# A's scores first, their maximum subtracted by VectorE: a scheduling change in a fused Nyström attention and SiLU layer

## The chip, the cores and the metric

The kernel runs on one core of a Trainium2 chip. A core has five engines with a queue each, and each works its queue in order: TensorE (PE; its weight loads are shown apart, as PEld), VectorE (DVE), ScalarE (ACT), GpSimd (POOL) and SyncE (SP). They meet at semaphores. Matrix products go to PSUM, 8 banks of 128 partitions x 2 KB, and VectorE and ScalarE fetch them from there. The metric is the device time of one execution in microseconds (us).

## The reference

Eight batches of eight heads, 576 tokens, 64 numbers a head. Keys and queries are averaged over 18 tokens each to 32 landmarks; three softmaxes come out of them, and the pseudo-inverse of the small one is found by six Newton steps. Heads are then joined to rows of 512, and one hidden layer of 2048 with SiLU follows:

```
q_lm, k_lm = mean over 18 tokens of q, k          # 32 landmarks a head
A  = softmax(scale * q    @ k_lm.T)               # 576 x 32
Bm = softmax(scale * q_lm @ k_lm.T)               # 32 x 32
C  = softmax(scale * q_lm @ k.T)                  # 32 x 576
Z  = Bm.T / (norm_1(Bm) * norm_inf(Bm) + 1e-6)
six times: Z = 2 Z - Z @ Bm @ Z
x  = A @ Z @ C @ v                                # heads joined: 4608 x 512
h  = x @ w_in;  out = (h / (1 + exp(-h))) @ w_out # 512 -> 2048 -> 512
```

## The kernel before, in words

The kernel is a hand-written order of instructions: what stands first in the program stands first in its engine's queue. It walks over batches b = 0 to 7, each in 16 steps s. In every step the hidden layer of batch b advances: `l1(s)` computes two blocks of 128 hidden columns for half of the tokens ("hps", four matmuls of 288 columns into one of two double banks), `act(s)` is ScalarE's SiLU from "hps" to "gT", and `l2_mm(n)` issues n matmuls of the output layer ("ops", 128x512). Sixteen of them make one output tile of 128 tokens; the sixteenth is followed by ScalarE's copy "ost" and a store from SP's queue. The tables CNT, EVEN and ODD say how many are issued in each step of batches 0 and 1, of even and of odd batches; they are the filling between the other work.

In the same 16 steps the attention of batch b + 1 is prepared by an object `a` (class Att). From b = 2 on this runs so:

- step 1: B's scores into columns 448 to 511 of a bank "bb" (`b_scores`), C's scores into both double banks "scp" (`c_scores`), their maxima on VectorE, the table of the exponential on ScalarE, and B's exponential `b_exp` ("pb");
- step 2: A's scores in five chunks of up to 128 tokens, two to a bank (`a_scores(0)`, `(1)`, `(2)`). `a_max` on VectorE writes the negated maximum of each row and head to "nm"; `a_shift` adds it to the scores by a matmul with the identity; `a_exp` on ScalarE writes the exponentials. Between them stand pieces of `l2_mm`. The last chunk has 64 tokens. At the end comes the table of SiLU;
- step 3: two pending `act`, the first products of the Newton steps (`f_mm`, `ns_mm`), which go on to step 8, one a step, with VectorE's part `ns_step`;
- step 6: C times v (`w_mm`), scaled into W; GpSimd multiplies A by its reciprocal sums, and SP's queue transposes it by DMA ("AT");
- steps 10 to 14: `z_mm` gives Z C v per head, and `m_pair` multiplies it by w_in ("mb"), the weights of the next batch's `l1`.

The first tile of A's scores lies in the one bank of the pool "a" (`psa1`, also used by `m_pair` and `w_mm`), the second in one of the two banks of pool "o" that "ops" uses, the third in columns 128 to 383 of "bb". GpSimd's queue loads q and k well ahead of their use (`load_qk`), one transfer for four heads of q or k, forms landmark sums, and copies the landmarks into block-diagonal form (`bd_expand`, in step 15).

Helpers record most instructions, so many have the line of a helper: every matmul has L77. The lines the text speaks of: L273 B's maximum, L286 B's exponential, L349 the first Newton scaling, L420 and L425 C's maximum and its scaling, L430 C's exponential, L545 A's maximum, L558 A's exponential, L651 and L652 the copies of `m_pair`, L685 SiLU, L711 "ost", L151 a change of ScalarE's table.

Of the kernel before, what the change touches and what calls it, by code (L numbers as in the profile page):

```python
# [8 lines left out]
FP = mybir.dt.float32  # L9
# [31 lines left out]
def kernel(  # L41
# [34 lines left out]
    def mm(o, lhsT, rhs, start, stop):  # L76
        nc.tensor.matmul(out=o, lhsT=lhsT, rhs=rhs, start=start, stop=stop,  # L77
                         skip_group_check=True)
# [19 lines left out]
    def load_qk(b, js=(1, 0, 3, 2)):  # L98
        if b not in nat_t:
            nat_t[b] = loadp.tile([128, 4, SEG * Dh], BF, tag="nat", name="nat")  # L100
        nat = nat_t[b]
        for j in js:
            src = (q, k)[j % 2]
            g = j // 2
            nc.gpsimd.dma_start(
                out=nat[:, j, :],
                in_=src[b, 4 * g:4 * g + 4].rearrange("h (l t) d -> (h l) (t d)", t=SEG))

    def load_v(b):
        vt = loadp.tile([VP, H, VC * Dh], BF, tag="v", name="v")  # L110
# [14 lines left out]
    nc.gpsimd.affine_select(out=ident_f, in_=ident_f, compare_op=OP.is_equal, fill=0.0,  # L125
                            base=0, pattern=[[-1, 128]], channel_multiplier=1)
# [96 lines left out]
    class Att:  # L223
        def __init__(self, b):
            self.b = b
            self.qkT, self.v, self.lmn = qkT_t[b], v_t[b], lmn_t[b]
            self.bd = bd_t[b % 2]


            self.tiled = b < 2  # L230
            self.by_dma = b >= 2

            self.mean = b <= 2

# [229 lines left out]
        def w_mm(self):  # L464
            vv = self.v.rearrange("p h (c d) -> p h c d", d=Dh)
            self.w = (psa1 if self.b else pso1)("wp")[:, 0:2 * Dh].rearrange("p (g d) -> p g d", d=Dh)
            for g in range(2):
                for c in range(VC):
                    for h in range(4):
                        p = slice(32 * h, 32 * h + 32)  # L470
                        mm(self.w[p, g, :], self.eCT[g][0:VP, c, self.quadrant(g, h)],
                           vv[:, 4 * g + h, c, :],
                           start=(c == 0 and g == 0), stop=(c == VC - 1))

        def w_out(self):
            self.W = attp.tile([128, 2, Dh], BF, tag="W", name="W", bufs=1)
            for g in range(2):
                nc.scalar.activation(out=self.W[:, g, :], in_=self.w[:, g, :], func=AF.Copy,
                                     scale=self.wsc[:, g:g + 1])


        def z_mm(self, bank=None):
            if self.tiled:

                self.zt = [self.bb[:, 320:384], bank[:, 0:64]]
                for g in range(2):
                    for h in range(4):
                        p, r = slice(32 * h, 32 * h + 32), h % 2
                        mm(self.zt[h // 2][64 * r:64 * r + 64, 32 * g:32 * g + 32],
                           self.W[p, g, :], self.x[p, g, :], start=(g == 0), stop=True)  # L490
                return
# [18 lines left out]
        def a_start(self):  # L510
            self.nm = attp.tile([128, len(TCH), 8], BF, tag="nm", name="nm")
            self.ex = attp.tile([128, len(TCH), 256], BF, tag="ex", name="ex")
            self.arec = attp.tile([128, len(TCH), 8], FP, tag="arec", name="arec")
            self.an = attp.tile([128, len(TCH), 256], BF, tag="an", name="an")
            self.AT = AT_t[self.b] = attp.tile([128, 2, S], BF, tag="AT", name="AT")

        def a_dims(self, i):
            cc = list(range(2 * i, min(2 * i + 2, len(TCH))))
            return cc[0], len(cc), TCH[cc[0]][1] - TCH[cc[0]][0]

        def a_scores(self, i):
            if i == 0:
                s = psa1("sa")
            elif self.b == 0:
                s = pso1("sa")
            else:
                s = pso1("sa") if i == 1 else self.bb[:, 128:384]
            self.sa[i] = s
            first = True
            for c in range(2 * i, min(2 * i + 2, len(TCH))):  # L530
                c0, c1 = TCH[c]
                o = 256 * (c - 2 * i)
                ov = s[0:c1 - c0, o:o + 256].rearrange("p (r g n) -> p g r n", r=2, g=2)
                for g in range(2):
                    for e in range(2):
                        mm(ov[:, g].rearrange("p r (j l) -> p r j l", l=L),
                           self.qkT[:, 2 * g, c0:c1, e],
                           self.bd[:, g, :, e].rearrange("p (j r l) -> p r j l", r=2, l=L),
                           start=first, stop=(e == 1))
                        first = False  # L540

        def a_max(self, i, eng=nc.vector):
# [38 lines left out]
        def a_mul(self, i):  # L581
            c, n, pr = self.a_dims(i)
            x, r = self.a_part(i)
            nc.gpsimd.tensor_tensor(  # L584
                out=self.an[0:pr, c:c + n, :].rearrange("p c (h l) -> p (c h) l", l=L), in0=x,
                in1=r.unsqueeze(2).to_broadcast((pr, 8 * n, L)), op=OP.mult)
            if self.by_dma:
                for m in range(c, c + n):
                    c0, c1 = TCH[m]
                    nc.sync.dma_start(out=self.AT[:, :, c0:c1], in_=self.an[0:pr, m, :],  # L590
                                      transpose=True)


        def a_transpose(self, k, bank=None):
# [98 lines left out]
    def l2_mm(n):  # L693

        st = l2_state
        while n > 0 and st["queue"]:
            b, c0 = st["queue"][0]
            if st["pos"] == 0:
                st["ps"] = pso1("ops")
            dc = st["pos"]  # L700
            tok = c0 + 127 - TL * (b % 2)
            assert acted[b] >= dc // 2 + (8 if tok >= SPLIT[b] else 0)
            mm(st["ps"], gT_t[b][:, dc, c0:c0 + 128], w_out_sb[:, dc, :],
               start=(dc == 0), stop=(dc == NDC - 1))
            st["pos"] += 1
            n -= 1
            if st["pos"] == NDC:
                st["queue"].pop(0)
                st["pos"] = 0
                ost = outp.tile([128, DM], FP, tag="ost", name="ost", bufs=3)  # L710
                nc.scalar.copy(out=ost, in_=st["ps"])  # L711
                r0 = S * b + c0 - TL * (b % 2)
                nc.sync.dma_start(out=out[r0:r0 + 128, :], in_=ost)
# [98 lines left out]
    for b in range(B):  # L812
# [11 lines left out]
        def act(s):  # L824
            l1_act(b, s, h.pop(s))

        for s in range(NDC):
# [248 lines left out]
```

## Time and profile before

| what | value |
|---|---|
| median of 3 runs (lowest, highest) | 272.93 us (272.14, 273.26) |
| profiled execution: its time, its span | 272.43 us, 270.7 us |
| PE busy | 259.6 us, 96% |
| PEld busy | 145.1 us, 54% |
| ACT busy | 177.0 us, 65% |
| DVE busy | 151.7 us, 56% |
| POOL busy | 117.9 us, 44% |
| mean DMA rate | 120 GB/s |

A span is the time from the first to the last instruction of the profiled execution; what lies around it is the launch's. Busy shares are means over the whole span. A group's line names the source line, the engine, the operation, output and input tiles and how often it ran; then busy time in all, the mean of one in ns, and the idle time of the engine just before it with what ended it. In lists in order of time the first two numbers are the start (us from the span's start) and the length.

### The profile page before, as it was taken

How to read it: one execution, taken by the hardware profiler on the slowest of the kernel's cores; microseconds unless marked ns; L12 is line 12 of the kernel's file. 1: busy time of each engine (PE TensorE's matmuls, PEld its weight loads, DVE VectorE, ACT ScalarE, POOL GpSimd, SP SyncE). 2: the span in 40 equal slices, each digit the busy share in tenths (PEclk: the TensorE clock that was granted, in tenths of full speed). 3: DMA queues.
4: the chain of work that ended last, by engine and by line, in shares of the span. 5: the costliest groups of instructions: out<-in, count | busy, mean ns of one | idle time of the engine just before them, and what ended most of it. 6: DMA issues, size and time to landing. Idle time of an engine off the chain costs nothing.

```text
span 270.7 us, 6824 instructions
## 1 busy us (share of the span) xinstructions
PE 259.6 (96%) x2785; PEld 145.1 (54%) x2785; DVE 151.7 (56%) x379; ACT 177.0 (65%) x339; POOL 117.9 (44%) x169
## 2 busy tenths in 40 slices
PE   6899899999999999999999999999999999999994
PEld 2647555475554555555646555556545554555541
DVE  4768893648585857746784658566775553100000
ACT  2367966769648964788678856697579756645611
POOL 8525427014996089353974299305951030100000
PEclk9999999999999999999999999999999999999999
DMA  6999999956994945659196938222291622121122
GB/s 105 201 209 207 206 206 220 210 109 111 203 128 106 170 122 71 139 85 181 58 119 134 204 94 131 85 68 70 29 182 42 99 60 63 39 80 39 39 80 77
DMA packets 37792, 32.36 MB, mean 120 GB/s; under 512 B 18817, under 2 KB 29057, under 8 KB 37761
## 3 DMA queue, kind: packets, MB, share of 16 engines
q0 software_dynamic: 15104, 18.35, 42.2%
q1 hardware_dynamic: 22656, 13.57, 21.4%
q8 instruction: 22, 0.36, 0.6%
q14 instruction: 10, 0.07, 0.1%
HBM read 36.70 MB, written 9.44 MB: 170 GB/s over the span
## 4 chain that ended last, share of the span: by engine, by line
PE 77%; DMA 12%; ACT 6%; POOL 2%; DVE 2%; issue 1%; ACTq 0%; POOLq 0%
PE ops L77 43%; PE hps L77 20%; DMA v<-in_v_dram 7%; PE bb L77 4%; PE sa L77 3%; DMA eCT<-eC 3%; DMA nat<-in_q_dram 2%; PE mp L77 2%; PE lmp L77 1%; ACT L151 1%; PE wp L77 1%; PE scp L77 1%; POOL w_out_sb L135 1%; PE mpp L77 1%; ACT ost L711 1%
## 5 line engine op out<-in xcount | busy, mean ns | idle before, releaser
L77 PE MATMUL ops<-w_out_sb,gT 128*128 128x512 bf16 x576 | 148.4, 380 | 0.0
L685 ACT ACTIVATE gT<-hps 128x576 bf16<-128x576 f32 (+2 forms) x128 | 82.5, 650 | 55.4 <-PE hps L77 55.1
L77 PE MATMUL hps<-AT,mb 128*128 128x288 bf16 (+2 forms) x512 | 82.5, 286 | 0.8 <-ACT gT L685 0.5
L77 PEld LDWEIGHTS <-gT 128*128 128x128 bf16 x576 | 52.9, 98 | 47.0 <-issue 5.4
L77 PEld LDWEIGHTS <-mb 128*128 128x128 bf16 x512 | 48.3, 98 | 26.8 <-issue 2.2
L182 DVE STREAM_TRANSPOSE qkT<-nat 128x576 f32<-128x576 f32 x32 | 39.0, 1244 | 1.5 <-DMA nat<-in_k_dram 1.2
L711 ACT COPY ost<-ops 128x512 f32<-128x512 f32 x36 | 21.1, 586 | 15.6 <-PE ops L77 14.7
L584 POOL TENSOR_TENSOR an<-ex,arec 128x512 bf16<-128x512 bf16 (+1 forms) x24 | 21.1, 901 | 19.5 <-DVE arec L574 16.4
L379 DVE SCALAR_TENSOR_TENSOR fx<-fx,bb 128x320 bf16<-128x320 bf16 (+1 forms) x39 | 17.1, 439 | 22.0 <-PE bb L77 21.3
L651 DVE CAST mb<-mp 128x512 bf16<-128x512 f32 x28 | 18.0, 686 | 11.5 <-PE mp L77 11.5
L208 POOL TENSOR_TENSOR lma<-nat 128x1152 f32<-128x1152 bf16 x10 | 23.7, 2372 | 0.0
L151 ACT ACT_TABLE_LOAD x16 | 20.5, 1283 | 1.1 <-PEq L1060 0.8
L978 POOL CAST gate<-fx 128x2 f32<-128x2 bf16 x6 | 1.1, 185 | 44.8 <-DVE fx L349 44.8
L254 POOL COPY bd<-lmc 32x128 bf16<-32x128 bf16 (+1 forms) x32 | 8.9, 280 | 25.4 <-DVE lmc L246 19.4
L77 PEld LDWEIGHTS <-fx 32*32 32x32 bf16 (+1 forms) x168 | 8.4, 93 | 11.8 <-DVE fx L379 1.9
L652 ACT CAST mb<-mpp 128x1024 bf16<-128x1024 f32 x14 | 14.2, 1011 | 0.0
L77 PEld LDWEIGHTS <-ident 128*128 128x128 bf16 (+2 forms) x194 | 9.6, 98 | 8.4 <-issue 4.2
L569 DVE TENSOR_REDUCE arec<-ex 128x16 f32<-128x512 bf16 (+1 forms) x24 | 14.0, 585 | 0.1
L77 PE MATMUL bb<-fx 32*32 32x64 bf16 (+2 forms) x168 | 13.1, 205 | 0.4
L689 POOL COPY gT<-gT 128x1024 bf16<-128x1024 bf16 x4 | 4.1, 1036 | 19.0 <-ACT gT L685 18.9
L420 DVE TENSOR_REDUCE cmx<-scp 128x1 f32<-128x576 f32 x16 | 11.9, 753 | 0.8 <-PE scp L77 0.5
L77 PEld LDWEIGHTS <-qkT 128*128 128x128 bf16 (+1 forms) x160 | 9.7, 99 | 4.9 <-DVE cbs L425 2.1
(104 smaller groups left out, 268.5 us busy)
## 6 DMA issues: line engine op xcount, KB each, us to landing
out_dram<-ost SPq DMA_DIRECT2D x36, 256.0 KB, 2.3
nat<-in_k_dram POOLq DMA_DIRECT2D x16, 288.0 KB, 7.0
nat<-in_q_dram POOLq DMA_DIRECT2D x16, 288.0 KB, 8.3
v<-in_v_dram POOLq DMA_DIRECT2D x8, 576.0 KB, 7.4
w_in_sb<-in_moe_w_in_dram POOLq DMA_DIRECT2D x4, 512.0 KB, 15.2
w_out_sb<-in_moe_w_out_dram POOLq DMA_DIRECT2D x4, 512.0 KB, 14.0
AT<-an SPq DMA_TRANSPOSE x30, 4.0
eCT<-eC SPq DMA_TRANSPOSE x12, 6.1
```

The costliest lines, as they stand in the source:

```text
L77: nc.tensor.matmul(out=o, lhsT=lhsT, rhs=rhs, start=start, stop=stop, skip_group_check=True)
L151: nc.scalar.activation(out=spare[:, 1:2], in_=spare[:, 0:1], func=func)
L182: nc.vector.transpose(out=o.rearrange("p (l t) -> p t l", t=SEG), in_=nat_t[b][:, j, :].bitcast(FP).rearrange("p (t l) -> p t l", l=L))
L208: nc.gpsimd.tensor_tensor(out=a1, in0=nat[:, :, 0:3 * w], in1=nat[:, :, 3 * w:6 * w], op=OP.add)
L379: nc.vector.scalar_tensor_tensor(out=n, in0=self.fx, scalar=2.0, in1=self.p, op0=OP.mult, op1=OP.add if self.tiled else OP.subtract)
L420: nc.vector.tensor_reduce(out=mx, in_=self.s[g][:, :, 0:HF], op=OP.max, axis=AX.XY, negate=True)
L569: nc.vector.tensor_reduce(out=r, in_=x, op=OP.add, axis=AX.X)
L584: nc.gpsimd.tensor_tensor(out=self.an[0:pr, c:c + n, :].rearrange("p c (h l) -> p (c h) l", l=L), in0=x, in1=r.unsqueeze(2).to_broadcast(( ...
L651: nc.vector.tensor_copy(out=o[:, r, 0:512], in_=m[r])
L652: nc.scalar.copy(out=o[:, :, 512:1024], in_=m2)
L685: nc.scalar.activation(out=gT_t[b][:, 2 * s:2 * s + 2, o + c0:o + c1], in_=h[:, :, 0:c1 - c0], func=AF.Silu)
L711: nc.scalar.copy(out=ost, in_=st["ps"])
```

## The change

From batch 3 on (the object of batch b + 1 in the loops b = 2 to 6) the shift by a matmul is gone. `a_sub` on VectorE adds the negated maximum to the scores on the way from PSUM to a float32 tile "xs" in SBUF, and one ScalarE instruction takes the exponential of all five chunks. A's first two tiles are scored in steps 0 and 1, ahead of B's and C's, and both in the bank of pool "a"; the third is scored at the start of step 2. The last chunk is scored over 128 tokens that overlap the chunk before, and only its second half is transposed into AT.

From batch 2 on a group of four heads is made of heads of one parity. W is written into two halves of a zeroed tile "wz", and z is two matmuls of 128 columns over the whole array in place of four of 64. EVEN and ODD are set anew. "zero" and "ident_f" take the place of later tiles.

```diff
@@ load_qk
-                in_=src[b, 4 * g:4 * g + 4].rearrange("h (l t) d -> (h l) (t d)", t=SEG))
+            if b < 2:
+                x = src[b, 4 * g:4 * g + 4].rearrange("h (l t) d -> (h l) (t d)", t=SEG)
+            else:
+                x = src[b].rearrange("(h g) (l t) d -> g h l (t d)", t=SEG, g=2)[g]
+            nc.gpsimd.dma_start(out=nat[:, j, :], in_=x)
@@ constants
-    zero = constp.tile([128, 512], BF, tag="zero", name="zero")
+    zero = outp.tile([128, DM], FP, tag="ost", name="zero", bufs=3).bitcast(BF)[:, 0:512]
-    ident_f = constp.tile([128, 128], FP, tag="ident_f", name="ident_f")
+    ident_f = nsp.tile([128, 128], FP, tag="lmd", name="ident_f", bufs=1)
+    wz = constp.tile([128, 2, 128], BF, tag="wz", name="wz")
+    nc.vector.memset(wz, 0.0)
@@ Att
+            self.sub = b >= 3
@@ z_mm
-                xv = xb[:, g, :].rearrange("p (j r l) -> p r j l", r=2, l=L)
-                for r in range(2):
-                    mm(self.zt[64 * r:64 * r + 64, 64 * g:64 * g + 64]
-                       .rearrange("p (j l) -> p j l", l=L),
-                       self.W[:, g, :], xv[:, r], start=(g == 0), stop=True)
+                mm(self.zt, wz[:, g, :], xb[:, g, :], start=(g == 0), stop=(g == 1))
@@ a_scores
-            if i == 0:
+            if i == 0 or self.sub and i == 1:
                 s = psa1("sa")
...
+                if self.sub:
+                    c0 = c1 - 128
@@ new
+        def a_sub(self, i):
+            c, n, pr = self.a_dims(i)
+            nc.vector.tensor_tensor(
+                out=self.xs[:, c:c + n, :].rearrange("p c (h l) -> p (c h) l", l=L),
+                in0=self.sa[i][:, 0:256 * n].rearrange("p (m l) -> p m l", l=L),
+                in1=self.nm[:, c:c + n, :].rearrange("p c h -> p (c h)").unsqueeze(2)
+                    .to_broadcast((128, 8 * n, L)), op=OP.add)
+        def a_exp_all(self):
+            nc.scalar.activation(out=self.ex, in_=self.xs, func=AF.Exp,
+                                 scale=sc if self.mean else sc / SEG)
@@ counts
-    EVEN = [1, 4, 11, 9, 5, 5, 5, 4] + [4] * 8
-    ODD = [4, 4, 12, 6, 3, 3, 2, 2] + [4] * 8
+    EVEN = [1, 2, 13, 10, 5, 4, 5, 4] + [4] * 8
+    ODD = [4, 2, 14, 8, 2, 2, 2, 2] + [4] * 8
@@ step 0
                 l1(s)
                 act(s)
+                if nxt and a.sub:
+                    a.a_start()
+                    a.a_scores(0)
+                    a.a_max(0)
+                    a.a_sub(0)
                 l2_mm(cnt[s])
@@ step 1
                 l1(s)
                 act(s)
+                if a.sub:
+                    a.a_scores(1)
+                    a.a_max(1)
+                    a.a_sub(1)
                 l2_mm(cnt[s])
...
                 a.b_scores()
                 a.c_scores()
                 a.b_max()
                 a.c_max(0)
                 table(AF.Exp)
...
                 a.b_exp()
@@ step 2
+            elif s == d + 2 and a.sub:
+                a.a_scores(2)
+                a.c_max(1)
+                a.a_max(2)
+                a.a_sub(2)
+                a.c_exp(0)
+                a.c_exp(1)
+                l2_mm(cnt[s])
+                a.a_exp_all()
+                a.b_norm()
+                table(AF.Silu)
+                l1(s)
```

More of the change, by code (lines that the diff above doesn't have):

```diff
@@ L104, in load_qk @@
             g = j // 2
-            nc.gpsimd.dma_start(
-                out=nat[:, j, :],
-                in_=src[b, 4 * g:4 * g + 4].rearrange("h (l t) d -> (h l) (t d)", t=SEG))
+            if b < 2:
[3 more added lines that the diff above has]
+            nc.gpsimd.dma_start(out=nat[:, j, :], in_=x)
     def load_v(b):
@@ L471, in w_mm @@
                         mm(self.w[p, g, :], self.eCT[g][0:VP, c, self.quadrant(g, h)],
-                           vv[:, 4 * g + h, c, :],
+                           vv[:, 2 * h + g if self.by_dma else 4 * g + h, c, :],
                            start=(c == 0 and g == 0), stop=(c == VC - 1))
         def w_out(self):
-            self.W = attp.tile([128, 2, Dh], BF, tag="W", name="W", bufs=1)
+            if not self.by_dma:
+                self.W = attp.tile([128, 2, Dh], BF, tag="W", name="W", bufs=1)
             for g in range(2):
-                nc.scalar.activation(out=self.W[:, g, :], in_=self.w[:, g, :], func=AF.Copy,
-                                     scale=self.wsc[:, g:g + 1])
+                nc.scalar.activation(
+                    out=wz[:, g, Dh * g:Dh * g + Dh] if self.by_dma else self.W[:, g, :],
+                    in_=self.w[:, g, :], func=AF.Copy, scale=self.wsc[:, g:g + 1])
         def z_mm(self, bank=None):
@@ L514, in a_start @@
             self.an = attp.tile([128, len(TCH), 256], BF, tag="an", name="an")
+            if self.sub:
+                self.xs = attp.tile([128, len(TCH), 256], FP, tag="xs", name="xs", bufs=1)
             self.AT = AT_t[self.b] = attp.tile([128, 2, S], BF, tag="AT", name="AT")
@@ L518, in a_dims @@
             cc = list(range(2 * i, min(2 * i + 2, len(TCH))))
-            return cc[0], len(cc), TCH[cc[0]][1] - TCH[cc[0]][0]
+            return cc[0], len(cc), 128 if self.sub else TCH[cc[0]][1] - TCH[cc[0]][0]
         def a_scores(self, i):
-            if i == 0:
+            if i == 0 or self.sub and i == 1:
                 s = psa1("sa")
@@ L531, in a_scores @@
                 c0, c1 = TCH[c]
+                if self.sub:
+                    c0 = c1 - 128
                 o = 256 * (c - 2 * i)
@@ L535, in a_scores @@
                     for e in range(2):
[L536 to L539, printed above, removed]
+                        if self.by_dma:
+                            mm(s[0:c1 - c0, o + 128 * g:o + 128 * g + 128],
+                               self.qkT[:, 2 * g, c0:c1, e], self.bd[:, g, :, e],
+                               start=first, stop=(e == 1))
+                        else:
+                            mm(ov[:, g].rearrange("p r (j l) -> p r j l", l=L),
+                               self.qkT[:, 2 * g, c0:c1, e],
+                               self.bd[:, g, :, e].rearrange("p (j r l) -> p r j l", r=2, l=L),
+                               start=first, stop=(e == 1))
                         first = False
@@ L589, in a_mul @@
                     c0, c1 = TCH[m]
-                    nc.sync.dma_start(out=self.AT[:, :, c0:c1], in_=self.an[0:pr, m, :],
-                                      transpose=True)
+                    nc.sync.dma_start(out=self.AT[:, :, c0:c1],
+                                      in_=self.an[pr - (c1 - c0):pr, m, :], transpose=True)
         def a_transpose(self, k, bank=None):
```

## The prediction

> **What bounds the kernel now.** I read the busy table of the page first, then the five stretches that the change touches, then the chain of waits and the order in time inside one of them.
>
> The busy table says that the chip is waiting for TensorE nearly all the time:
>
> ```profile
> PE 259.6 (96%) x2785; PEld 145.1 (54%) x2785; DVE 151.7 (56%) x379; ACT 177.0 (65%) x339; POOL 117.9 (44%) x169
> ```
>
> The stage in question runs from the first hidden-layer product of step 0, l1(0), to that of step 4, l1(4), in the loops b = 2 to 6. The busy times by stretch (length, then PE, PEld, DVE, ACT, POOL) for b = 2, for b = 4 (even) and b = 5 (odd):
>
> ```profile
> 84.78:95.85 11.07, 10.75 (x125) 5.95 (x118) 7.19 (x22) 10.42 (x22) 3.08 (x7) 1.00 0.95 159
> 144.48:155.06 10.58, 10.58 (x118) 5.95 (x116) 5.99 (x20) 9.86 (x21) 3.19 (x7) 1.00 0.96 152
> 174.75:185.95 11.20, 10.96 (x119) 6.06 (x117) 6.20 (x21) 9.59 (x21) 1.93 (x4) 1.00 0.30 82
> ```
>
> PE is never idle in the even stage and 0.24 us in the odd one; the clock is full. ScalarE is nearly as full (9.86 of 10.58). So work taken from PE is worth its length, and any new wait on PE costs its length. The chain of waits inside the even stage (start, length, what):
>
> ```profile
> 146.91 0.52 PE scp L77 x28
> 147.43 1.03 PE sa L77 x16
> 148.46 1.29 PE ops L77 x6
> 149.75 0.35 PE bb L77 x4
> 150.10 0.32 PE sa L77
> 150.43 0.43 PE ops L77 x2
> 150.86 0.22 PE sa L77
> 151.07 0.43 PE ops L77 x2
> 151.50 0.22 PE bb L77
> ```
>
> 16 score matmuls take 1.03, so 0.065 each; an ops matmul 0.215. The two "sa" and the last "bb" are the shifts that the change removes. The order in time shows the engines that answer:
>
> ```profile
> 147.95 0.27 ACT L286 ACTIVATE pb<-bb,bbs 128x32 f32<-128x32 f32 x1
> 148.38 0.20 ACT L286 ACTIVATION_READ_ACCUMULATOR pb<-bb,bbs 128x1 f32 x1
> 149.20 1.28 DVE L545 TENSOR_REDUCE nm<-sa 128x16 bf16<-128x512 f32 x2
> 149.68 0.26 PEld L77 LDWEIGHTS <-qkT 128*64 128x64 bf16 x4 [0.42 <-DVE cbs L425]
> 152.13 0.58 ACT L711 COPY ost<-ops 128x512 f32<-128x512 f32 x1
> 152.73 1.28 ACT L151 ACT_TABLE_LOAD   x1
> 154.14 1.17 ACT L685 ACTIVATE gT<-hps 128x576 bf16<-128x576 f32 x2
> ```
>
> The reader sees that between maximum and exponential PE always has ops to do. And a group table gives prices:
>
> ```profile
> L349 DVE TENSOR_TENSOR fx<-bb,nrm 128x256 bf16<-128x256 f32 x6 | 2.5, 424 | 4.4 <-PE bb L77 4.4
> L651 DVE CAST mb<-mp 128x512 bf16<-128x512 f32 x28 | 18.0, 686 | 11.5 <-PE mp L77 11.5
> L545 DVE TENSOR_REDUCE nm<-sa 128x16 bf16<-128x512 f32 x16 | 10.3, 682 | 0.1
> ```
>
> **What is removed.** Per changed batch (five of them) PE loses the shifts: in the raw starts 150.03 to 150.26, 150.69 to 150.91, and from the end of the ops before (151.34) to 151.66, so 0.23 + 0.22 + 0.32. The third score tile goes from 128x64 weights to 128x128: 149.59 to 150.03 becomes 4 x 0.065 = 0.26, 0.18 less. Together 0.95. z takes two 128-column matmuls without a change of tile size in place of four 64-column ones: 194.46 to 194.73 becomes about 0.11, 0.16 less in each of six batches (0.96 in all). Three exponentials on ScalarE (1.18 for two and 0.38) become one of 1280 columns; from 256 columns 0.381 and 512 columns 0.597 it is 0.84 ns a column, so 1.25.
>
> **What is added.** VectorE gets three subtractions. No row shows this operation. From L349 (0.424 at 256 columns from PSUM) and the cast (0.686 at 512) I take 0.69 and 0.42. Ends: 0.60 (the spacing of two maxima, 1.28 less 0.68) and, for a float32 result in SBUF, the far row of the 576-column float32 transposition, 1.25, scaled to 512: 1.1.
>
> **What is moved.** A's scores come first. The first two score tiles now share the one buffer of the "a" pool, so the second waits until the first has been subtracted. VectorE's queue becomes max 0, sub 0, max 1, sub 1, and only then B's maximum. The third tile lies in the bank of B's scores and comes right behind C's scores; in the built program its first matmul carries a wait on VectorE (B's maximum) and on ScalarE (B's exponential). In the kernel before it carries the same waits, but six ops (1.29) and 16 score matmuls (1.03) stood ahead of it.
>
> Walk of an even stage, zero at l1(0), latencies from rows: PE's last matmul to the next engine 0.2 (hps to 193.10, gT from 193.30), VectorE to a weight load 0.06 and its matmul 0.16 (L349 ends 185.23, matmul 185.40), ScalarE to PE 0.09.
>
> - l1(0) to 0.49, scores 0 to 1.01, one ops to 1.23, l1(1) to 1.72. VectorE: max 0 from 1.20 to 1.89, sub 0 to 2.61. Scores 1 start at 2.77: PE waits 1.05.
> - Scores 1 to 3.29. VectorE: max 1 from 3.48, sub 1 to 4.88, B's maximum and its scaling (0.23 and 0.17) to 5.27, ScalarE's two exponentials (147.95 to 148.58, 0.63) to 5.98. PE meanwhile: two ops, then B's and C's scores (0.83 with the change of tile size) to 4.55. Scores 2 start at 6.04: PE waits 1.49.
> - Scores 2 to 6.30, 13 ops to 9.10, l1(2) and l1(3) to 10.08, two ops, f_mm, eight ops and the first Newton product: ready for l1(4) at 12.47.
> - ScalarE: C's exponentials end near 8.1. Ops 13 ends a group of 16, and its copy "ost" is queued ahead of the big exponential: 9.35 to 9.93 (0.25 after PE, as at 152.13), exponential to 11.18, table load to 12.48, act(2) 12.61 to 13.26. l1(4) needs that buffer: 13.35, another 0.88.
>
> Before, the same stretch took 10.58, with one ops less (0.215): 10.80. An even batch loses 2.55 (two of them). b = 2 starts 0.28 later, since the tile buffer is freed by the copy of "mp", and its old stage was 11.07 + 0.215 = 11.29: 2.34. Odd batches have four ops between scores 0 and l1(1), so the first wait is 0.41; 14 ops then end the group at 9.31 and l1(4) starts at 13.56, against 11.20 + 2 x 0.215 = 11.63: 1.93 (two of them). Sum 2.34 + 5.10 + 3.86 = 11.30, less 0.96 for z: +10.3.
>
> The profiled execution took 272.43 (its span of 270.7 and 1.7 around it), so 282.7 for its like; the median of the three runs is 0.5 higher, 272.93, and against it the forecast is 283.2, as are the times below.
>
> That the third tile waits although it writes other columns (128 to 383) than B's scores (448 to 511) is what the row at 149.68 hints at, a weight load released by VectorE; but PE was busy until 149.66 there, so the row proves no cost. [...]
>
> **Costed at nothing.** B's diagonal copies on GpSimd end at 144.73 (143.46 + 1.27) and scores 0 now want them at 144.97: 0.24 of cover; later copies would move the whole walk. The loads by head parity keep their count and their row length, are issued in 0.55 each and are used a batch later. The new memset (L161's like, 0.165) lies in front of a wait of VectorE for GpSimd's identity (1.2). "zero" and "ident_f" sharing buffers are read last long before those are needed. C's transposed exponentials leave ScalarE near 8.1 instead of 5.7; with a landing of 4.4 (8.8 at most) they are there by 12.5 to 16.9, and w_mm wants them at about 16 to 17: covered, barely at the worst.
>
> **Rivals.**
> - ScalarE's end is hidden (the copy goes early, or the exponential from SBUF is shorter): l1(4) at 12.47, odd 12.26. Losses 1.46 + 2 x 1.67 + 2 x 0.62 = 6.0, less 0.96: 278.0. Against it: ScalarE was already 9.86 of 10.58 busy.
> - The third tile is not held (B's exponential early enough): the walk then gives l1(4) at 12.07 and 12.12, losses 1.06 + 2 x 1.27 + 2 x 0.49 = 4.6, less 0.96: 276.5. Against it: VectorE's queue order.
> - The other side: VectorE's answer is covered by PE's work. From the end of scores 0 to scores 2 the answer takes 5.03, and PE has 2.49 of work there (even), 3.13 (odd). If it were below that, the stages would be 9.93 and 10.36 long: 1.36 + 2 x 0.87 + 2 x 1.27 + 0.96 = 6.6 gained, 266.3. It decides at an answer of 3.4 (even) to 4.4 (odd), where the wait eats the stage's gain of 0.87 or 1.27. For it: PE's load falls for sure. Against it: two maxima alone measured 1.28, and the subtractions cannot be free.
> - The subtraction is as slow as the far row, 1.1: 0.82 more per batch, 287.3.
>
> **Chances.** Forecast 0.62, ScalarE hidden 0.12, third tile not held 0.06, slow subtraction 0.07, the other side 0.10, near nothing 0.03. The range goes from just below the rival at 276.5 to the slow one: 276.0 to 287.5. A difference of 0.5% (1.4 us) is what a measurement can tell from none; faster 0.10, same 0.03, slower 0.87.
>
> **What would show it.** Right: PE's weight loads wait for the subtraction's output "xs" about 1.0 in even and 0.4 in odd batches; PE's "bb" for ScalarE's "pb" about 1.5, five times; l1(4) for "gT" about 0.9 to 1.3; PE's share falls to about 93%. Wrong: no such waits, "xs" well under 0.6, or ScalarE's table load ending by 11.5 after l1(0). What would make the prediction wrong above all is a shorter answer of VectorE than these rows give.

## Result, and the profile after

The changed kernel takes 299.02 us (median of six executions, 297.42 to 302.35), the kernel before 272.96 beside it on the same chip: a ratio of 1.0955, with a 95% interval of 1.0893 to 1.1016. It is slower, as forecast, but by 26 us where the forecast had 10.3, and 11.5 us above the top of the range. The profiled execution is the one of 297.42 us, its span 295.7; it stands against the 272.43 and 270.7 of before, so 25.0 us are to be found.

From the page of the changed kernel, the busy table, the granted clock in 40 slices, the queue of GpSimd's transfers (packets, MB, share of the 16 DMA engines) and three groups of transfers (how many, KB, median us from issue to landing):

```profile
PE 254.4 (86%) x2717; PEld 146.2 (49%) x2758; DVE 161.6 (55%) x395; ACT 176.2 (60%) x329; POOL 121.1 (41%) x169
...
PEclk9997999999859999999999999999999999999999
...
q0 software_dynamic: 24320, 18.39, 44.9%
...
eCT<-eC SPq DMA_TRANSPOSE x12, 8.4
...
nat<-in_k_dram POOLq DMA_DIRECT2D x16, 288.0 KB, 12.5
nat<-in_q_dram POOLq DMA_DIRECT2D x16, 288.0 KB, 14.1
```

The same four lines of the kernel before:

```profile
q0 software_dynamic: 15104, 18.35, 42.2%
...
nat<-in_k_dram POOLq DMA_DIRECT2D x16, 288.0 KB, 7.0
nat<-in_q_dram POOLq DMA_DIRECT2D x16, 288.0 KB, 8.3
...
eCT<-eC SPq DMA_TRANSPOSE x12, 6.1
```

TensorE's share falls from 96% to 86%: the loss is waiting, not work. In slice 4 (22 to 30 us) and slices 11 and 12 (74 to 89 us) the granted clock is below full (0.7, 0.8 and 0.5 of it). And GpSimd's queue moves nearly the same bytes in more packets: 24320 against 15104 before. The loads of q and k ("nat") land in 12.5 and 14.1 us; before it was 7.0 and 8.3.

The trace gives the start of every l1. Length of the stretches in us, before and after:

| batch | l1(0) to l1(8), before | after | rest of the batch, before | after |
|---|---|---|---|---|
| 1 | 16.83 | 16.83 | 13.84 | **25.59** |
| 2 | 18.27 | 20.15 | 12.49 | 12.31 |
| 3 | 16.46 | 19.90 | 12.49 | 12.31 |
| 4 | 17.78 | 19.99 | 12.49 | 12.31 |
| 5 | 16.46 | 18.02 | 12.49 | 12.31 |
| 6 | 17.78 | 19.97 | 12.49 | 12.31 |

Two more rows make the sum whole: batch 1 begins 2.85 later (0.5 to 2.2 in the runs below that leave the loads of four heads in a row uncut, 2.85 to 5.5 in the three with the loads of the changed kernel), and batch 7 is as long as before. 2.85 + 11.75 + 1.88 + 3.44 + 2.21 + 1.56 + 2.19 - 5 x 0.18 = 24.98. Of the 2.85, 1.60 stand ahead of the first l1 of all, around which the clock of slice 4 is low. The run below with the load of batch 4 five steps later has the same program up to there, and neither that delay nor that clock, so these 1.60 us belong to this execution and not to the change.

So there are two losses. One is the loss forecast, about 2 us in each of b = 2 to 6. The other, 11.75 us at one place in b = 1 and about 1.9 more in b = 3 (19.90 where the other odd batch has 18.02), was forecast nowhere. The same stretches as in the prediction, in the changed kernel (length, then PE, PEld, DVE, ACT, POOL, the granted clock, the DMA share, GB/s); the first row is the long one in b = 1:

```profile
73.78:99.37 25.59, 14.64 (x154) 8.07 (x155) 10.74 (x24) 8.20 (x14) 12.46 (x18) 0.80 0.95 101
99.37:112.53 13.16, 10.27 (x120) 5.82 (x115) 9.53 (x27) 9.97 (x20) 4.38 (x6) 1.00 0.91 124
164.05:177.02 12.97, 10.13 (x114) 5.88 (x114) 8.32 (x25) 9.41 (x19) 4.69 (x7) 1.00 0.94 115
196.35:209.54 13.19, 10.57 (x116) 6.09 (x116) 8.74 (x25) 9.41 (x19) 3.16 (x4) 1.00 0.27 71
```

In the even stage (third row) PE has less to do, 10.13 against 10.58, and yet the stage is 2.4 longer: 2.84 us of idle time where there was none. The order in time inside it, with the idle time ahead of an instruction and what ended it in brackets:

```profile
166.67 0.63 PE L77 MATMUL sa<-bd,qkT 128*128 128x128 bf16 x8 [0.81 <-DVE xs L574]
...
168.07 0.69 DVE L574 TENSOR_TENSOR xs<-sa,nm 128x512 f32<-128x512 f32 x1
168.68 0.21 DVE L281 TENSOR_REDUCE bmx<-bb 128x2 f32<-128x64 f32 x1
...
169.88 0.39 PE L77 MATMUL bb<-bd,qkT 128*128 128x128 bf16 x4 [1.43 <-ACT pb L294]
...
173.16 0.58 ACT L740 COPY ost<-ops 128x512 f32<-128x512 f32 x1 [1.46 <-issue]
...
173.65 1.27 ACT L582 ACTIVATE ex<-xs 128x1280 bf16<-128x1280 f32 x1
...
174.94 1.28 ACT L153 ACT_TABLE_LOAD   x1
...
177.02 0.41 PE L77 MATMUL hps<-AT,mb 128*128 128x288 bf16 x2 [0.55 <-ACT gT L714]
```

These are the three waits of the walk, each at its place: scores 1 for the subtraction, scores 2 for B's exponential behind VectorE's queue, l1(4) for ScalarE, which stood still for 1.46 us ahead of the copy and only then began the large exponential.

The other loss, in b = 1: PE and the queue of transposes (SP), in order of time.

```profile
75.27 0.65 PE L77 MATMUL hps<-AT,mb 128*128 128x288 bf16 x4
84.31 0.51 PE L77 MATMUL wp<-v,eCT 96*32 96x64 bf16 x24 [8.39 <-DMA eCT<-eC]
86.85 0.51 PE L77 MATMUL wp<-v,eCT 96*32 96x64 bf16 x24 [2.02 <-DMA eCT<-eC]
87.69 1.49 PE L77 MATMUL ops<-w_out_sb,gT 128*128 128x512 bf16 x3 [0.33 <-issue]
```

```profile
66.88 7.50 SPq L445 DMA_TRANSPOSE eCT<-eC  x2
74.43 1.07 SPq L742 DMA_DIRECT2D out_dram<-ost  x2
78.44 14.02 SPq L619 DMA_TRANSPOSE AT<-an  x5
```

In the kernel before, SP's queue had the pair at:

```profile
64.03 4.52 SPq L437 DMA_TRANSPOSE eCT<-eC  x2
```

w_mm, C times v, waits for the transposes of C's exponentials, which SP issued at 66.88 and which landed at 84.3 and 86.8. They share the time with the load of q and k for batch 4, whose rows move from 66.5 to 83.0. Before, the pair had landed at 72.9 and 73.5, and w_mm stood 0.20 us for the second: in b = 1 there was no cover to begin with.

### The profile page after: what moved, and what is told of

Its sections match the earlier page's. It is cut to its first block, busy times and chain, and to the rows that moved or that the text cites. A ratio compares the mean times of both kernels' runs of the same rounds, so it can differ in the third digit from the quotient of the medians.

```text
span 295.7 us, 6725 instructions
## 1 busy us (share of the span) xinstructions
PE 254.4 (86%) x2717; PEld 146.2 (49%) x2758; DVE 161.6 (55%) x395; ACT 176.2 (60%) x329; POOL 121.1 (41%) x169
## 3 DMA queue, kind: packets, MB, share of 16 engines
q0 software_dynamic: 24320, 18.39, 44.9%
## 4 chain that ended last, share of the span: by engine, by line
PE 59%; DMA 19%; DVE 8%; ACT 6%; issue 5%; POOL 2%; POOLq 0%; ACTq 0%
PE ops L77 32%; PE hps L77 17%; DMA eCT<-eC 9%; DMA v<-in_v_dram 7%; DMA nat<-in_q_dram 3%; DVE nm L561 3%; DVE xs L574 2%; PE bb L77 2%; PE sa L77 2%; DVE cmx L428 2%; ACT L153 2%; ACT ex L582 2%; PE mp L77 2%; PE wp L77 1%; PE mpp L77 1%
## 5 line engine op out<-in xcount | busy, mean ns | idle before, releaser
L77 PE MATMUL ops<-w_out_sb,gT 128*128 128x512 bf16 x539 | 139.8, 381 | 3.6 <-issue 2.4
L613 POOL TENSOR_TENSOR an<-ex,arec 128x512 bf16<-128x512 bf16 (+2 forms) x24 | 21.2, 902 | 35.8 <-DVE arec L603 31.9
L561 DVE TENSOR_REDUCE nm<-sa 128x16 bf16<-128x512 f32 (+1 forms) x17 | 11.2, 672 | 13.0 <-PE sa L77 12.9
L77 PEld LDWEIGHTS <-qkT 128*128 128x128 bf16 (+1 forms) x160 | 10.3, 98 | 14.6 <-issue 4.9
L77 PE MATMUL wp<-v,eCT 96*32 96x64 bf16 x384 | 5.1, 201 | 13.0 <-DMA eCT<-eC 12.1
L681 ACT CAST mb<-mpp 128x1024 bf16<-128x1024 f32 x14 | 14.2, 1011 | 0.0
L598 DVE TENSOR_REDUCE arec<-ex 128x16 f32<-128x512 bf16 (+2 forms) x24 | 14.1, 586 | 0.1
L77 PE MATMUL sa<-bd,qkT 128*128 128x128 bf16 (+1 forms) x132 | 10.2, 220 | 2.8 <-DVE xs L574 2.7
## 6 DMA issues: line engine op xcount, KB each, us to landing
nat<-in_k_dram POOLq DMA_DIRECT2D x16, 288.0 KB, 12.5
nat<-in_q_dram POOLq DMA_DIRECT2D x16, 288.0 KB, 14.1
```

What stands on the lines that cost most here:

```text
L561: eng.tensor_reduce(out=self.nm[0:pr, c:c + n, :], in_=self.sa[i][0:pr, 0:256 * n].rearrange("p (c h l) -> p c h l", h=8, l=L), op=OP.max, ...
L598: nc.vector.tensor_reduce(out=r, in_=x, op=OP.add, axis=AX.X)
L613: nc.gpsimd.tensor_tensor(out=self.an[0:pr, c:c + n, :].rearrange("p c (h l) -> p (c h) l", l=L), in0=x, in1=r.unsqueeze(2).to_broadcast(( ...
L681: nc.scalar.copy(out=o[:, :, 512:1024], in_=m2)
```

## The experiments

The first four took the change apart; three more tested what came out of that; the last four were about the loads.

**The subtraction alone.** The loads, the heads and z as before, all the rest as changed (the columns in which A's scores are written go with the heads, and are as before too):

```diff
-                x = src[b].rearrange("(h g) (l t) d -> g h l (t d)", t=SEG, g=2)[g]
+                x = src[b, 4 * g:4 * g + 4].rearrange("h (l t) d -> (h l) (t d)", t=SEG)
...
-                           vv[:, 2 * h + g if self.by_dma else 4 * g + h, c, :],
+                           vv[:, 4 * g + h, c, :],
...
-                mm(self.zt, wz[:, g, :], xb[:, g, :], start=(g == 0), stop=(g == 1))
+                xv = xb[:, g, :].rearrange("p (j r l) -> p r j l", r=2, l=L)
+                for r in range(2):
+                    mm(self.zt[64 * r:64 * r + 64, 64 * g:64 * g + 64]
+                       .rearrange("p (j l) -> p j l", l=L),
+                       self.W[:, g, :], xv[:, r], start=(g == 0), stop=True)
```

> The subtraction part alone: from batch 3 VectorE subtracts, A is scored first, new counts; the quads, the loads and z are those of the kernel before. Theory L (the loads by head parity are slow and hold up C's transposed exponentials): the stall of batch 1 (11.75 us more between steps 8 and 16 of b = 1) and the 2.85 us lost up to b = 1 go, the stages of b = 2 to 6 stay 1.9 to 2.4 us longer each; 272.4 + about 8.5 + 0.96 for the old z: 281 to 283 us, and the clock stays full. Rival S (the new order itself makes C's exponentials late): w_mm goes on waiting for eCT, 295 us or more.

282.42 us, ratio 1.035 (1.0324 to 1.0376). The stages from l1(0) to l1(4) in b = 2 to 6 are 13.17, 13.20, 12.98, 13.20 and 12.99 long, those of the changed kernel to 0.01; the long stretch in b = 1 is 13.52. All three waits of the walk are this part's.

**The head parity alone.** The kernel before with the loads, the order of heads in w_mm and in the columns of A's scores, "wz" and the two products of z from the changed one:

```diff
-            nc.gpsimd.dma_start(
-                out=nat[:, j, :],
-                in_=src[b, 4 * g:4 * g + 4].rearrange("h (l t) d -> (h l) (t d)", t=SEG))
+            if b < 2:
+                x = src[b, 4 * g:4 * g + 4].rearrange("h (l t) d -> (h l) (t d)", t=SEG)
+            else:
+                x = src[b].rearrange("(h g) (l t) d -> g h l (t d)", t=SEG, g=2)[g]
+            nc.gpsimd.dma_start(out=nat[:, j, :], in_=x)
...
+                mm(self.zt, wz[:, g, :], xb[:, g, :], start=(g == 0), stop=(g == 1))
```

> The quads by head parity alone: the loads, w_mm's heads, wz and the two whole-array z matmuls; shifts, order and counts of the kernel before. Theory L: 272.4 + 2.85 + 11.75 - 0.96 for z, about 286 us, with w_mm of b = 1 waiting 8 us or more for eCT, landings of nat of 11 us and more, and 9216 more packets in the software queue. Rival S: 271.5 to 273 us, no wait for eCT.

295.66 us, ratio 1.0808 (1.0768 to 1.0847): direction as expected, size not. The part that was costed at nothing is the dear one. w_mm waits for "eCT" in b = 1 (26.87 for the stretch), in b = 3 (2.99 and 0.49) and b = 4 (1.17 and 0.22), and in b = 0 for v, which shares GpSimd's queue with the loads (2.5). The two parts do not add up, 9.5 + 22.7 being more than 26: the changed kernel waits for "eCT" only 1.07 and 0.58 in b = 3 and not at all in b = 4. That the waits for the subtraction push w_mm back there, and so cover what is late, is my reading; it was not tried by itself.

**One head in a transfer.** Each load of four heads at a stride cut into four loads of one head, 16 in a batch:

```diff
-                x = src[b].rearrange("(h g) (l t) d -> g h l (t d)", t=SEG, g=2)[g]
-            nc.gpsimd.dma_start(out=nat[:, j, :], in_=x)
+                for h in range(4):
+                    nc.gpsimd.dma_start(
+                        out=nat[32 * h:32 * h + 32, j, :],
+                        in_=src[b, 2 * h + g].rearrange("(l t) d -> l (t d)", t=SEG))
```

> The changed kernel with each load by head parity cut into four transfers of one head (32 rows to 32 partitions), so that no transfer has heads at a stride. Theory L1 (the strided form of one transfer is slow: the three small packets a row): the extra packets are nearly gone, landings fall back to about 7 us, 281 to 284 us; GpSimd issues 16 transfers a batch at 0.55 us in place of 4, which costs it 6.6 us a batch, off the path. Theory L2 (the heads' order in memory is slow, whatever the form): landings stay at 11 us or more and the time at 295 to 300 us.

297.28 us, ratio 1.088 (1.0858 to 1.0903): hardly any gain in time, but the loss has moved. The loads land in 3.7 and 4.1 us, w_mm no longer stands for "eCT", and the stretch in b = 1 is 14.34; but b = 0 has grown by 10.8 from l1(4) to l1(8), and the stage of b = 2 by 3.0 (2.2 of it a wait for GpSimd's "bd"). The waits of this kernel from 36 to 56 us:

```profile
PE atp L638 <- POOL an L616: 8.8, 2, 8.6
POOL nat L110 <- DMA w_out_sb<-in_moe_w_out_dram: 4.1, 2, 2.1
POOL nat L110 <- DMA v<-in_v_dram: 2.6, 1, 2.6
```

GpSimd's own queue is the new wait. The loads stand in it ahead of A's normalising product "an"; three of them wait until an earlier transfer (w_out, v) has landed, and "an" waits behind them. The semaphores in the trace say which one: the program gives GpSimd's transfers eight semaphores in turn, and the issue of a transfer waits for the one eight issues before it. Every issue that was held up for over 0.5 us starts 0.28 to 0.29 us after the landing of that one, in this run and in the kernel before. With 16 loads in a batch it is still on its way. One wait less was paid with another.

**The large exponential ahead of the copy.** The subtraction alone, with a_exp_all queued before the output products:

```diff
-                l2_mm(cnt[s])
                 a.a_exp_all()
+                l2_mm(cnt[s])
```

> As the run with the subtraction part alone, but the one big exponential is queued on ScalarE ahead of the copy ost of step 2. By the walk of the prediction l1(4) then no longer waits for act(2): 0.88 us an even and 1.3 us an odd stage less, 5.2 us in all, so 276 to 278 us where the run without it gives 281 to 283. Rival: the next wait (f_mm and the first Newton product behind VectorE) takes its place at once, less than 1.5 us gained.

278.5 us, ratio 1.0191 (1.0164 to 1.0217), 3.9 less, where 5.2 were expected. The stages are 12.45, 12.05, 12.27, 12.05 and 12.27. So ScalarE's late start was 0.7 to 1.15 of each stage, and not 0.88 to 1.3.

**A's tiles in two banks again.** On the subtraction alone: scores 1 in a bank of the pool "o" as before the change, placed behind l1(1) and B's scores, so that it waits for no subtraction; VectorE's order max 0, sub 0, B's maximum, max 1, sub 1; the exponential in two parts (four chunks, then one); six or four output products between C's scores and scores 2.

```diff
-            if i == 0 or self.sub and i == 1:
+            if i == 0:
...
-    EVEN = [1, 2, 13, 10, 5, 4, 5, 4] + [4] * 8
-    ODD = [4, 2, 14, 8, 2, 2, 2, 2] + [4] * 8
+    EVEN = [0, 6, 10, 10, 5, 4, 5, 4] + [4] * 8
+    ODD = [0, 4, 16, 8, 2, 2, 2, 2] + [4] * 8
...
                 a.b_scores()
+                a.a_scores(1)
                 a.c_scores()
                 a.b_max()
+                a.a_max(1)
+                a.a_sub(1)
...
                 a.b_exp()
+                l2_mm(cnt[s])
+                a.a_exp_part(0, 4)
```

> The subtraction with q and k loaded as before, but A's first two tiles in two banks again (pool a and pool o), C's scores behind them, the exponential in two parts (four chunks, then the last) and the output matmuls set anew (EVEN 0, 6, 10; ODD 0, 4, 16), so that PE never waits for a subtraction to free a bank and ScalarE starts the first part while VectorE is still busy. Theory (VectorE's answer and ScalarE's order set the stage, not the subtraction as such): from VectorE's queue 1.2 + 5.8 us of maxima and subtractions end at 7.0 after l1(0), the last exponential at 7.5, the copy and the table at 9.4, act(2) at 10.1, l1(4) at about 10.2 to 10.5, against 12.05 to 12.45 in the run with the exponential first: 268.5 to 272. Rival (the 5.8 us of VectorE are too many however they are ordered): the stages stay over 11.3 long and the time over 274.

270.03 us, ratio 0.9875 (0.9839 to 0.9911): a little faster than the kernel before, by 1.2%. Its stages of b = 2, 4 and 5:

```profile
85.67:96.08 10.41, 10.25 (x121) 5.96 (x115) 8.82 (x25) 10.17 (x21) 3.14 (x7) 1.00 0.95 153
144.76:154.93 10.17, 10.01 (x114) 6.00 (x114) 7.62 (x23) 9.61 (x20) 3.20 (x7) 1.00 0.97 156
174.41:185.45 11.04, 10.49 (x117) 6.21 (x116) 7.72 (x23) 9.19 (x20) 2.03 (x4) 1.00 0.32 85
```

PE is idle for 0.16 us of the even stage. VectorE still takes every maximum and every subtraction (7.62 busy, 8.32 in the longer stage of the changed kernel), so they were never too much for it; the order and the shared bank were what PE waited for. The run changes the bank, the order, the counts and the exponential together, so what each of them is worth is not shown. From l1(0) to l1(8) the five batches take 17.40, 16.71, 17.16, 15.87 and 17.16, 2.45 less in all than before the change.

**Only the form of the loads undone.** The changed kernel with the one line of the loads as it was before.

```diff
-                x = src[b].rearrange("(h g) (l t) d -> g h l (t d)", t=SEG, g=2)[g]
+                x = src[b, 4 * g:4 * g + 4].rearrange("h (l t) d -> (h l) (t d)", t=SEG)
```

> The changed kernel with one line undone: the loads of q and k take four heads in a row again, all the rest (scores, wz, z over the whole array, subtraction) as in the changed kernel. The heads are then paired with the wrong heads, so its output is not the reference's; the work is the same. Theory (the strided form of the loads is all of the 14 us that the subtraction alone does not explain): the run of the subtraction alone, 282.4, less 0.16 for z in each of six batches: 281.5 (280.8 to 282.3); no wait of w_mm for eCT in step 9 of b = 1. Rival (z over the whole array or the other order of heads in the products costs): over 286.

281.38 us, ratio 1.0307 (1.0269 to 1.0344). That one line is 17.6 of the 26 us by the medians, and 14.9 between the two profiled executions (spans of 295.7 and 280.9): 12.3 in b = 1, 1.9 in b = 3 and 0.7 ahead of b = 1, which is in the spread of that stretch. The remaining 8.46 are the subtraction's waits less the gain of z.

**The load of batch 4 five steps later.**

```diff
-                if s == (5 if b == 1 else 1) and b + 3 < B:
+                if s == (10 if b == 1 else 1) and b + 3 < B:
                     load_qk(b + 3)
```

> The changed kernel, only the load of q and k for batch 4 is issued in step 10 of b = 1, behind the transposes of C's exponentials and w_mm, not in step 5. The strided loads stay. Theory (the transposes of C's exponentials land late because the strided load is in flight at that time): steps 8 to 16 of b = 1 go from 25.6 to about 14 and the time from 299 to 286 to 288; the smaller wait in b = 3 stays. Rival (the transposes are late by themselves, or any strided load in the batch delays them): steps 8 to 16 stay over 20 and the time over 294.

296.31 us, ratio 1.0817 (1.0758 to 1.0876), so about 9 us short of the theory. The wait for "eCT" in b = 1 is gone: with no load in flight the pair landed in 2.9 and 2.8 us, where the changed kernel has 17.4 and 17.9. But the transposes of A, which come next from the same queue, now collide with the load; the first l1 of b = 2 needs them. From the waits of its profiled execution:

```profile
PEld L77 <- DMA AT<-an: 11.3, 1, 11.3
PE hps L77 <- DMA AT<-an: 10.9, 1, 10.9
```

(That execution took 302.5, the longest of the four; the place of the wait is read from it, not its length, and no shorter one was profiled.) The first half of the theory holds: what is late is what is in flight together with such a load. Its second half, that step 10 is a time at which nothing else is, does not.

**116 and 12 rows, and 112 and 16 rows.** What makes the strided form slow? In the built programs a load before reads 128 rows at one distance; the changed one reads 4 blocks of 32 rows. Two theories stood against each other: the stride itself, or the 4. 116 and 12 rows divide by 4 and by no higher power of two, 112 and 16 both by 16, and none of them has a stride. The subtraction alone, each load of four heads in a row cut in two:

```diff
-            nc.gpsimd.dma_start(
-                out=nat[:, j, :],
-                in_=src[b, 4 * g:4 * g + 4].rearrange("h (l t) d -> (h l) (t d)", t=SEG))
+            x = src[b, 4 * g:4 * g + 4].rearrange("h (l t) d -> (h l) (t d)", t=SEG)
+            for p, r in ((0, 128),) if b < 2 else ((0, 116), (116, 128)):
+                nc.gpsimd.dma_start(out=nat[p:r, j, :], in_=x[p:r])
```

> The subtraction alone, q and k loaded four heads in a row as before, but from batch 2 on each of these transfers is cut into one of 116 rows and one of 12 rows. No stride between heads, as many bytes and rows. In the changed kernel the outermost dimension of a load is 4 (heads at a stride), and 8 of 16 packets on average were in flight in the load of b = 1, against 14 before. [...] The rival that the stride itself is what is slow (its small packets, three for a row) expects the run to be like the subtraction alone, 282.4 to 284.5, with 14 packets in flight. [...]

> The control of the run with 116 and 12 rows: cut into 112 and 16 rows, both divisible by 16, so as many transfers and issues of GpSimd. Both theories expect 282.4 to 284.5; anything slower would be the price of the four more issues in a batch, and is to be taken off the other run.

293.32 (ratio 1.0711, 1.0642 to 1.0779) and 294.02 (1.0769, 1.0691 to 1.0847). The control was to take 282.4 to 284.5 and did not, so that the other run came out within the 290 to 299 expected if the 4 counts is luck: both kernels lose 7.8 us in b = 0 and about 4 in b = 1, and in b = 0 it is GpSimd's queue again, with "an" behind the loads (PE waits 5.9 and 6.2 for it) and the loads behind the transfer eight issues before. The pair still answers its question, since its two runs do not differ measurably: the rows of a plain block go out as fast when their number has only 4 as a large divisor (loads landed in 6.3 and 7.3) as when it has 16 (6.1 and 6.5).

**128 rows at one stride, and 16 blocks of 8 rows.** As many transfers as before, so GpSimd's queue is left out of it:

```diff
-                in_=src[b, 4 * g:4 * g + 4].rearrange("h (l t) d -> (h l) (t d)", t=SEG))
+                y = src[b].rearrange("h (l t) d -> (h l) (t d)", t=SEG)
+                x = y.rearrange("(a w) n -> w a n", w=2)[g]            # the one run
+                x = y.rearrange("(a w c) n -> w a c n", w=2, c=8)[g]   # the other
```

> The subtraction alone, with as many transfers, rows and bytes as before, but from batch 2 on each load of q or k takes every second of 256 rows: 128 single rows at one stride. The rows then go to other places than their own, so the output is not the reference's; the work is the same. The runs with 116 and 12 and with 112 and 16 rows came out alike (293.3 and 294.0) and slow for another reason, GpSimd's queue with its four more issues, so the divisors of a plain block of rows do not matter. Left are: a stride as such; the split of the rows into blocks (two levels of address, with its three small packets for a row); or that there are only 4 blocks. A stride as such expects the same late transposes as in the changed kernel, 295 or more; the two others expect 282.4 (281.5 to 283.5), as for the subtraction alone.

> As the run with every second row, but each load takes 16 blocks of 8 rows at a stride, where the changed kernel takes 4 blocks of 32. The rows go to other places than their own again. If the number of blocks sets how many rows are in flight at once (4 blocks few, 16 blocks all), this run is like the subtraction alone, 282.4 (281.5 to 284), with some 14 packets in flight in the load of b = 1. If the split into blocks is slow whatever their number, it is like the changed kernel: some 9984 small packets, few rows in flight, the transposes late, 293 to 300.

282.1 (ratio 1.0342, 1.0317 to 1.0367) and 282.71 (1.0352, 1.0321 to 1.0383): both like the subtraction alone. Neither a stride nor a split into blocks costs anything that these runs show; what is left is that there are only 4 blocks, of 32 rows each. From the page of the run with 16 blocks:

```profile
q0 software_dynamic: 15104, 18.35, 40.5%
...
nat<-in_k_dram POOLq DMA_DIRECT2D x16, 288.0 KB, 6.7
nat<-in_q_dram POOLq DMA_DIRECT2D x16, 288.0 KB, 8.0
...
eCT<-eC SPq DMA_TRANSPOSE x12, 4.6
```

Worked out from the packet records for the load issued in b = 1 (q and k of batch 4: four transfers, 512 rows of 2304 bytes; rows in flight are the sum of the packets' times over the length):

| kernel | length of the load, us | rows in flight | 4-byte packets in all | eCT's longest landing, us | time, us |
|---|---|---|---|---|---|
| before | 8.4 | 13.8 | 768 | 8.8 | 272.9 |
| subtraction alone | 8.0 | 14.5 | 768 | 8.6 | 282.4 |
| changed, only the loads as before | 7.7 | 14.9 | 768 | 8.2 | 281.4 |
| every second row | 7.5 | 15.1 | 768 | 8.1 | 282.1 |
| 16 blocks of 8 | 8.5 | 13.5 | 768 | 9.1 | 282.7 |
| changed, 4 blocks of 32 | 16.6 | 8.2 | 9984 | 17.9 | 299.0 |
| head parity alone, 4 blocks of 32 | 17.0 | 8.3 | 9984 | 18.6 | 295.7 |

This is the slowest load of the changed kernel. Its six loads in blocks of 32 took 9.1 to 16.6 us with 8.2 to 14.8 rows in flight; the same six loads took 7.1 to 9.1 us with 13.1 to 14.2 before the change. So the form lengthens every one of them, but few rows in flight do not follow from the form alone.

Why the load in 4 blocks had 8.2 rows in flight and the one in 16 blocks 13.5 is not shown: no trace here tells which engine took a row.

## Why the prediction was right, and where it was wrong

*The waits of the walk: right, most of them a little too long.* In the even stage scores 1 was to wait 1.05 and waited 1.11 (its weights) or 0.81 (the product); scores 2 was to wait 1.49 and waited 1.43; l1(4) was to wait 0.88 and waited 0.55. It was to come at 13.35 and came at 12.97, in odd batches at 13.19 for 13.56, in b = 2 at 13.16 for 13.63. The waits of the whole changed kernel (us in total, how often, the longest):

```profile
PE bb L77 <- ACT pb L294: 7.3, 6, 1.4
...
PEld L77 <- DVE xs L574: 4.3, 5, 1.1
...
PE hps L77 <- ACT gT L714: 3.6, 5, 1.0
```

The sum of these steps was +10.3, and with the loads left as they were the change costs +8.46. From l1(0) to l1(8), where the changed counts of output products cancel out, the five stages of that run lose 1.88, 1.56, 2.19, 1.56 and 2.19, which is 9.38 for the 11.30 of the sum. The 0.38 that each stage is short of the walk came in small pieces ahead of ScalarE's end: scores 2 started at 5.83 for 6.04, l1(2) at 8.87 for 9.10, the copy at 9.11 for 9.35.

*The prices: right.* The subtraction and the one large exponential, 0.69 and 1.25 in the prediction, measured 0.691 and 1.272:

```profile
L574 DVE TENSOR_TENSOR xs<-sa,nm 128x512 f32<-128x512 f32 x10 | 6.9, 691 | 0.3
...
L582 ACT ACTIVATE ex<-xs 128x1280 bf16<-128x1280 f32 x5 | 6.4, 1272 | 0.0
```

z was to gain 0.16 in a batch and gains 0.18.

*The third tile held by B's exponential: right.* It writes columns 128 to 383, B's scores lie in 448 to 511 of the same bank, and it waits 1.43 us for "pb". The built program carries that wait; whether the chip needs it, no run asked. Without it the sum would have been the rival's 4.6 less 0.96, +3.6, against the 8.46 measured with the loads left as they were.

*The step that failed* is under "Costed at nothing": "The loads by head parity keep their count and their row length, are issued in 0.55 each and are used a batch later." All three were true or nearly so (the issue takes 0.67), and beside the point. The step asked when the loads are used, and not what they hold up while they are in flight. The loads of four blocks move the same rows in 9.1 to 16.6 us in place of 7.1 to 9.1; the one of b = 1 takes 16.6 for 8.4, and the transposes in flight beside it take as long. With that the next sentence failed too: "with a landing of 4.4 (8.8 at most)" took the worst landing of before as the worst there can be (and 4.4 is the median of four landings in b = 4 and 5; over the whole trace it is 6.1). It was 17.9, w_mm waited 8.39 and 2.02, and from 79.8 to 90 us the clock granted to TensorE was 0.50. And cover was sought only in the batches whose order changes: in b = 1, whose order is as before, w_mm already stood 0.20 us for "eCT". Undoing the one line of the loads took 17.6 us off again. None of the rivals had this mechanism, and so the range ended at 287.5.

*The other side* had a chance of 0.10 as a measured outcome of this kernel and did not come about; but its mechanism, VectorE's answer covered by PE's work, is real. The run with two banks is that rival put to work: 270.03, where it was priced at 266.3 for every wait gone and the 0.96 of z gained, which this run leaves out.

What stays open: why strided loads of 4 blocks bring three 4-byte packets for each row (9984 - 768 = 9216 = 24 loads x 128 rows x 3), and whether those packets or the few rows in flight delay the transposes. Both come and go together in the runs of the table. The start of b = 1 also moved by 0.5 to 2.2 us in runs that leave the loads as they were. In the two of them that moved most (1.25 and 2.18) the granted clock was 0.50 once for 3.4 us ahead of b = 1, as in slice 4 of the changed kernel; why it was so in some executions and not in others is open.

## What to carry to other kernels

A transfer whose count, bytes and row length stay the same can still change its cost when its address pattern does (16.6 us for 8.4 here): look at how many blocks it reads (4 of 32 rows took 16.6 us, 16 of 8 rows 8.5), and at what else is in flight while it runs, on other queues too. When a load is cut up or moved to mend that, look at what stands behind it in the issuing queue, how many transfers the program lets be on their way (eight from GpSimd's queue here) and what its new neighbours are; here the same 10 us came back as GpSimd's queue in one run and as A's transposes in another. And when an engine takes over work from the bottleneck, the order of its answers can count for more than their length: the same subtractions cost 9.5 us in one order and gained 2.9 in another, with the bank, the counts and the exponential arranged to suit.

## What the runs showed of the hardware that was not expected

- Four loads of 128 rows each, as 4 blocks of 32 at a stride, had 8.2 rows in flight and took 16.6 us in b = 1; as 16 blocks of 8 at a stride 13.5 and 8.5 us; as 128 rows at one stride 15.1 and 7.5.
- Beside a load in 4 blocks on GpSimd's queue the transposes on SP's queue were late: the pair of "eCT" took 7.50 us from SP (4.52 before) and up to 17.9 to land (8.8 before); with no load in flight it landed in 2.9.
- After the waits of 8.39 and 2.02 us the clock granted to TensorE was 0.50, and it came back within a few us of work. The stretches 84.00 to 87.30, 87.30 to 90.00 and 90.00 to 94.00 of the changed kernel; the column ahead of the last two is the clock:

```profile
84.00:87.30 3.30, 0.97 (x48) 0.72 (x49) 0.00 (x0) 0.00 (x0) 0.00 (x0) 0.50 1.13 202
87.30:90.00 2.70, 2.37 (x14) 1.33 (x11) 0.52 (x2) 0.52 (x2) 0.00 (x0) 0.50 1.30 194
90.00:94.00 4.00, 4.00 (x27) 2.34 (x26) 3.90 (x10) 2.49 (x4) 3.26 (x3) 0.99 0.31 51
```

  The clock fell at 79.8, 3.9 us after the end of the last product before the wait, and was full again at 90.05, 3.2 us after the second half of w_mm began.
